# First stage: seven subtractions from VectorE to GpSimd, and transposes between the tiles on TensorE

## The chip, the cores and the metric

One NeuronCore of a Trainium2 chip runs the whole program. The metric is the device time in microseconds. The kernel before took 994.47 us (median of 3 runs, 994.19 to 994.80).

## The reference

The input is x, 2048 rows by 576 columns, f32. It is normalized over each row, goes through a 2-D real Fourier transform, is multiplied with complex weights, transformed back and added to x; then comes a second normalization, a wide layer of 4608 with ReLU, and a second addition.

```python
def _A_ref(x, w_r, w_i):
    X = jnp.fft.rfft2(x, axes=(-2, -1))
    X = X * (w_r + 1j * w_i)
    return jnp.fft.irfft2(X, s=(S, D), axes=(-2, -1))
def _B_ref(x, w1, w2):
    h = jnp.einsum("bsd,df->bsf", x, w1)
    return jnp.einsum("bsf,fd->bsd", jnp.maximum(h, 0), w2)
h = x + _A_ref(_layernorm(x), A_w_r, A_w_i)
h2 = h + _B_ref(_layernorm(h), B_w1, B_w2)
```

## The kernel before, in words

The rows are 16 tiles of 128 x 576. The program is written out in order, and each engine runs its instructions in the order in which they stand. There are four stages: the first (0 to 41 us of the span) normalizes, folds and makes the first step of the transform; the middle one (41 to 104 us) finishes the forward transform, multiplies and begins the inverse; then come the inverse with the second normalization, and the wide layer, nearly all of it matmuls.

The first stage is what the change touches. Its tiles go in 11 groups (`parts`, L237): tiles 0 to 3 alone, then the pairs 4-5, 6-7, 8-9, 10-11 and 12-13, then 14 and 15 alone. The steps of a group g are:

- `stat1` (L239, `ln_stats` L211): VectorE takes bn_stats (L215) and bn_aggr (L216) of x; GpSimd makes mean and scale out of them with three kinds of small instructions (L218 add, L219 power, L221 multiply, one for each tile). Below these are called the statistics block of a group.
- `norm1` (L243): ScalarE writes the normalized tile z (L229).
- `fold` (L251): VectorE adds z to its mirror image (L258, columns 1 to 288 of the buffer G), subtracts (L259, columns 289 to 576), and doubles column 0 by adding it to itself (L260).
- `fwd_a` (L264), for each tile: TensorE runs 12 matmuls (24 instructions in the trace, since each f32 matmul is done in two) into a PSUM buffer `d`, of which there are four. The first 4 matmuls (h = 0) read G's columns 0 to 255, all from the addition and the doubling; the next 4 (h = 1) read columns 320 to 575, from the subtraction; the last 4 (`rest`) read columns 256 to 319, from both. ScalarE copies the result to the buffer `A` (`act`, L158).

The loop at L301 sets the order: for g it writes stat1(g + 3), fold(g + 1), norm1(g + 2), then fwd_a of g's tiles. So on GpSimd the statistics block of g + 3 stands ahead of whatever fold(g + 1) puts there. Ahead of the loop stand 36 transposes of the identity (`warm_pe`, L289, L292), of which nothing is read; 8 and 12 more stand at the end of the middle stage. `mm` (L155) is the helper of all matmuls up to the inverse, so most of them have line L155. When the middle stage has read `A` for the last time, x is loaded again into the same memory (L449).

Of the kernel before, what the change touches and what calls it, by code (L numbers as in the profile page):

```python
# [13 lines left out]
ALU = mybir.AluOpType  # L14
# [14 lines left out]
GW = D + 2  # L29
# [93 lines left out]
def dims(ap, off, *pairs):  # L123

    return bass.AP(tensor=ap.tensor, offset=ap.offset + off, ap=[list(ap.ap[0]), *[list(p) for p in pairs]])
# [3 lines left out]
def kernel(ctx: ExitStack, tc: tile.TileContext, x, w_r, w_i, w1, w2, cc2, c1, fb, ib, c3, out):  # L129
    nc = tc.nc  # L130
# [5 lines left out]
    def sb(shape, tag, bufs=1, dt=F32):  # L136
        n[0] += 1
        return pool.tile(shape, dt, tag=tag, name=f"{tag}_{n[0]}", bufs=bufs)
# [3 lines left out]
    def ps():  # L142
        n[0] += 1
        if banks:
            return banks[0].tile([128, 1024], F32, tag="w", name=f"w_{n[0]}", bufs=2)
        return psum.tile([128, 1024], F32, tag="d", name=f"d_{n[0]}", bufs=4)
# [3 lines left out]
    def ebuf(shape, dt=F32):  # L150
        e = sb([128, EW], "e", EB, dt)[:, :int(np.prod(shape[1:]))]
        return e.rearrange("p (a b) -> p a b", a=shape[1]) if len(shape) == 3 else e

    def mm(o, l, r, start, stop):
        nc.tensor.matmul(o, l, r, start=start, stop=stop)  # L155

    def act(o, i, **kw):
        nc.scalar.activation(o, i, AF.Copy, **kw)  # L158
# [9 lines left out]
    ident = sb([128, 128], "ident")  # L168
# [82 lines left out]
    def fold(g):  # L251
        if g >= len(parts):
            return
        t0, k = parts[g]
        z = zin.pop(g)
        G = ebuf([128, 2, GW])
        a, b = dims(z, 1, [D, k], [287, 2], [1, 144]), dims(z, 575, [D, k], [-287, 2], [-1, 144])
        nc.vector.tensor_add(dims(G, 2, [GW, k], [-1, 2], [2, 144]), a, b)  # L258
        nc.vector.tensor_sub(dims(G, 575, [GW, k], [1, 2], [-2, 144]), a, b)  # L259
        nc.vector.tensor_add(G[:, :k, 0], z[:, :k, 0], z[:, :k, 0])  # L260
        for i in range(k):
            Fs[t0 + i] = G[:, i, :]

    def fwd_a(t):  # L264
        G = Fs.pop(t)
        p = ps()

        def rest(p):
            for e in range(2):
                for j in range(2):  # L270
                    q = slice(64 * j, 64 * j + 64)
                    mm(p[64 * e:64 * e + 64, 512 * j + 256:512 * j + 320], G[q, 256:320], caf[q, :64], True, True)

        end = t == NT - 1
        if end:
            p2 = ps()
            rest(p2)
            nc.vector.tensor_copy(dims(zx, 8192 + 2 * t, [32, 64], [1, 2]), dims(p2, 256, [1, 64], [512, 2]))
        for h in range(2):
            for k in range(2):  # L280
                for j in range(2):
                    q = slice(64 * j, 64 * j + 64)
                    mm(p[:, 512 * j + 128 * h:512 * j + 128 * h + 128], dims(G[q], (k, 321 - k)[h], [2, 128]),
                       caf[q, 64 * k:64 * k + 128], k == 0, k == 1)
        if not end:
            rest(p)
        act(dims(zx, 2 * t, [2048, 5 - end], [32, 64], [1, 2]), dims(p, 0, [64, 5 - end], [1, 64], [512, 2]))
# [9 lines left out]
    norm1(0)  # L297
    stat1(2)
    fold(0)
    norm1(1)  # L300
    for g in range(len(parts)):  # L301
        stat1(g + 3)
        fold(g + 1)
        norm1(g + 2)
        for t in range(parts[g][0], parts[g][0] + parts[g][1]):
            fwd_a(t)
# [844 lines left out]
```

## Time and profile before

| | us |
|---|---|
| median of 3 runs | 994.47 |
| the profiled execution's own time | 994.43 |
| its span, first to last instruction | 992.6 |
| TensorE busy, all stages | 972.9 |
| VectorE busy | 762.9 |
| ScalarE busy | 457.1 |
| GpSimd busy | 585.0 |
| first matmul of the middle stage starts at | 40.92 |
| in the first 41 us: TensorE, VectorE, ScalarE, GpSimd busy | 33.1, 28.1, 24.9, 19.5 |

PE is TensorE, DVE VectorE, ACT ScalarE, POOL GpSimd, SP the engine that issues most DMAs. In a row of the timeline stand the start, the duration, engine, line, operation, what is written and read, the count, and in brackets how long the engine was idle ahead of it and what ended that. PEclk is the granted clock of TensorE as a share of full speed.

### The profile page before, as it was taken

What the parts mean: (1) busy time and instruction counts of PE and PEld (TensorE: products, weight loads), DVE (VectorE), ACT (ScalarE), POOL (GpSimd) and SP (SyncE); (2) the same over time, 40 slices, a digit from 0 to 9 for tenths busy, and PEclk for the clock granted to TensorE, in tenths of its full rate; (3) what the DMA queues carried; (4) which work ended last, traced back from release to release, by engine and by line L of the source; (5) the groups of instructions that cost most, each with busy time, mean ns of one, the idle gap of its engine ahead of it and who ended that gap; (6) DMA issues with size and microseconds to landing.
All of it is one profiled execution on the core that took longest, in us unless ns stands there. A gap on an engine that the chain in (4) does not pass through costs nothing.

```text
span 992.6 us, 18029 instructions
## 1 busy us (share of the span) xinstructions
PE 972.9 (98%) x6708; PEld 863.1 (87%) x6708; DVE 762.9 (77%) x1185; ACT 457.1 (46%) x870; POOL 585.0 (59%) x730
## 2 busy tenths in 40 slices
PE   6999999999999999999999999999999999999997
PEld 6887668999998899999999999999999999999997
DVE  6688877437654878888888888878888888888886
ACT  5544364512323544544454554544454544544541
POOL 4300375602235867687767777687767777687741
PEclk8999999999999999999999999999999999999999
DMA  9952723466598472818264462819274563819365
GB/s 222 239 149 80 167 94 96 150 203 223 197 315 287 178 240 79 294 45 299 82 237 151 168 227 92 293 32 312 67 251 138 181 206 113 273 46 319 103 210 144
DMA packets 122727, 178.71 MB, mean 180 GB/s; under 512 B 7568, under 2 KB 102288, under 8 KB 122640
## 3 DMA queue, kind: packets, MB, share of 16 engines
q1 hardware_dynamic: 121904, 176.67, 55.4%
q8 instruction: 53, 0.87, 0.4%
q10 hardware_dynamic: 736, 0.89, 0.3%
q14 instruction: 34, 0.28, 0.1%
HBM read 153.15 MB, written 23.07 MB: 178 GB/s over the span
## 4 chain that ended last, share of the span: by engine, by line
PE 92%; DVE 4%; DMA 2%; ACT 1%; SPq 1%; issue 1%; DVEq 0%
PE h L784 33%; PE w L889 33%; PE d L155 24%; DMA A<-in_A_x_dram 2%; DVE st L215 1%; PE d L536 1%; PE w L155 1%; DMA X<-in_A_x_dram 1%; DVE A L899 0%; SPq L166 0%; DVE A L494 0%; PE h L889 0%; DVE D L600 0%; DVE mv L216 0%; ACT D L599 0%
## 5 line engine op out<-in xcount | busy, mean ns | idle before, releaser
L899 DVE TENSOR_TENSOR A<-A,w 128x576 f32<-128x576 f32 x415 | 307.3, 752 | 83.4 <-PE w L889 70.6
L889 PE MATMUL w<-X,D 128*128 128x288 f32 x1416 | 217.3, 295 | 0.5 <-ACT e L603 0.4
L889 PEld LDWEIGHTS w<-X,D 128*128 128x128 f32 x1416 | 204.4, 188 | 10.5 <-ACT e L603 0.6
L784 PE MATMUL h<-B,e 128*128 128x512 f32 x630 | 160.4, 393 | 0.9 <-DVE A L593 0.9
L158 ACT ACTIVATE e<-h 128x512 f32<-128x512 f32 x90 | 53.9, 599 | 184.4 <-PE h L784 184.4
L784 PEld LDWEIGHTS h<-B,e 128*128 128x128 f32 x630 | 113.3, 188 | 21.0 <-ACT e L158 1.1
L334 POOL TENSOR_TENSOR e<-e,e 128x512 fp32r<-128x512 f32 (+3 forms) x61 | 78.4, 1285 | 57.9 <-ACT e L158 52.7
L784 PE MATMUL h<-X,e 128*128 128x512 f32 x420 | 106.1, 392 | 0.0
L603 ACT ACTIVATE e<-e 128x512 f32<-128x512 f32 x90 | 57.0, 633 | 105.8 <-DVE e L842 46.6
L334 POOL TENSOR_TENSOR X<-e,X 128x576 fp32r<-128x576 f32 (+1 forms) x32 | 46.9, 1468 | 73.5 <-ACT X L158 73.5
L784 PEld LDWEIGHTS h<-X,e 128*128 128x128 f32 x420 | 75.7, 188 | 12.8
L158 ACT ACTIVATE e<-e 128x256 fp32r<-128x256 f32 (+5 forms) x162 | 74.5, 489 | 23.1 <-DMA t1T<-e 11.2
L808 POOL TENSOR_TENSOR A<-e 128x256 f32<-128x256 f32 x59 | 46.4, 787 | 27.4 <-DVE X L798 27.4
L798 DVE TENSOR_TENSOR D<-A,D 128x512 fp32r<-128x512 f32 x59 | 60.9, 1032 | 0.9 <-ACT D L158 0.9
L889 PEld LDWEIGHTS w<-X 128*128 128x128 f32 x360 | 53.8, 188 | 5.6 <-issue 0.7
L889 PE MATMUL w<-X 128*128 128x288 f32 x360 | 57.0, 294 | 0.5 <-DVE A L899 0.5
L889 PE MATMUL w<-X,e 128*128 128x288 f32 x348 | 55.5, 295 | 0.0
L155 PE MATMUL d<-e,D 128*128 128x288 f32 x384 | 53.4, 296 | 0.0
L155 PEld LDWEIGHTS d<-e,D 128*128 128x128 f32 x384 | 52.4, 188 | 1.1 <-issue 0.2
L784 PE MATMUL h<-C,e 128*128 128x512 f32 x210 | 53.3, 393 | 0.0
L784 PE MATMUL h<-F,e 128*128 128x512 f32 x210 | 53.2, 392 | 0.0
L810 POOL TENSOR_TENSOR A<-e,A 128x256 f32<-128x256 f32 x59 | 51.2, 868 | 0.8 <-DVE A L806 0.8
(164 smaller groups left out, 1863.3 us busy)
## 6 DMA issues: line engine op xcount, KB each, us to landing
X<-t0T SPq DMA_DIRECT2D x16, 768.0 KB, 8.0
X<-t1T SPq DMA_DIRECT2D x16, 768.0 KB, 7.8
e<-in_B_w_dram SPq DMA_DIRECT2D x18, 576.0 KB, 3.8
e<-in_B_w_dram SPq DMA_DIRECT2D x18, 512.0 KB, 3.9
X<-t0T SPq DMA_DIRECT2D x16, 512.0 KB, 8.6
X<-t1T SPq DMA_DIRECT2D x16, 512.0 KB
B<-t0T SPq DMA_DIRECT2D x8, 768.0 KB
F<-t0T SPq DMA_DIRECT2D x8, 768.0 KB
```

The costliest lines, as they stand in the source:

```text
L155: nc.tensor.matmul(o, l, r, start=start, stop=stop)
L158: nc.scalar.activation(o, i, AF.Copy, **kw)
L215: nc.vector.bn_stats(st[:, i, h, :], xs[:, t0 + i, 288 * h:288 * h + 288])
L334: eng.tensor_sub(l, v, h)
L536: nc.tensor.transpose(pz[:, 128 * ORDER[b]:128 * ORDER[b] + 128], y[:, 128 * b:128 * b + 128], ident)
L603: nc.scalar.activation(o, i, AF.Relu)
L784: nc.tensor.matmul(o, a, b, start=bool(first) and n_ == 0, stop=n_ == len(ops) - 1, skip_group_check=not first)
L798: (eng or nc.vector).tensor_sub(f[1], v, f[0])
L808: nc.gpsimd.tensor_sub(s3, p0[:, :256], p0[:, 256:])
L810: nc.gpsimd.tensor_sub(s4, p1_[:, :256], s2)
L889: nc.tensor.matmul(P[tt], l[:, q], r, start=first and n_ == 0, stop=end and n_ == 2, skip_group_check=whole and not first)
L899: nc.vector.tensor_add(xt, xt, P)
```

## The change

The subtraction of a fold goes to GpSimd in the first seven groups (tiles 0 to 9) and stays on VectorE in the other four. Column 0 is doubled by a multiplication with 2.0, which now stands ahead of the subtraction. And ahead of the matmuls of each of the tiles 1 to 11, TensorE gets four transposes of the identity into columns of the tile's PSUM buffer that nothing reads.

```diff
         nc.vector.tensor_add(dims(G, 2, [GW, k], [-1, 2], [2, 144]), a, b)
-        nc.vector.tensor_sub(dims(G, 575, [GW, k], [1, 2], [-2, 144]), a, b)
-        nc.vector.tensor_add(G[:, :k, 0], z[:, :k, 0], z[:, :k, 0])
+        nc.vector.tensor_scalar(G[:, :k, 0], z[:, :k, 0], 2.0, None, op0=ALU.mult)
+        (nc.gpsimd if g < 7 else nc.vector).tensor_sub(dims(G, 575, [GW, k], [1, 2], [-2, 144]), a, b)
         for i in range(k):
             Fs[t0 + i] = G[:, i, :]
...
+        if 1 <= t < 12:
+            for _ in range(4):
+                nc.tensor.transpose(p[:, 320:448], ident, ident)
         end = t == NT - 1
```

On GpSimd, before, the statistics blocks of the pairs 6-7 (r_284), 8-9 (r_318) and 10-11 (r_352) follow each other:

```order
L218 TENSOR_SCALAR r_284<-mv_283 128x2
L219 TENSOR_TENSOR r_284<-r_284,half_143 128x2
L221 TENSOR_SCALAR r_284<-mv_283,r_284 128x1 x2
L218 TENSOR_SCALAR r_318<-mv_317 128x2
L219 TENSOR_TENSOR r_318<-r_318,half_143 128x2
L221 TENSOR_SCALAR r_318<-mv_317,r_318 128x1 x2
L218 TENSOR_SCALAR r_352<-mv_351 128x2
```

After, at the same place (pair 6-7 is r_288, 8-9 r_326, 10-11 r_364; L260 is now the subtraction, e_299 the folded tile 3, e_337 the folded pair 4-5):

```order
L218 TENSOR_SCALAR r_288<-mv_287 128x2
L219 TENSOR_TENSOR r_288<-r_288,half_143 128x2
L221 TENSOR_SCALAR r_288<-mv_287,r_288 128x1 x2
L260 TENSOR_TENSOR e_299<-e_266 128x2x144
L218 TENSOR_SCALAR r_326<-mv_325 128x2
L219 TENSOR_TENSOR r_326<-r_326,half_143 128x2
L221 TENSOR_SCALAR r_326<-mv_325,r_326 128x1 x2
L260 TENSOR_TENSOR e_337<-e_303 128x2x2x144
L218 TENSOR_SCALAR r_364<-mv_363 128x2
```

Between every two statistics blocks there is now a subtraction, and the subtraction of tile 3 stands ahead of the block of 8-9, that of 4-5 behind it.

On TensorE, before, tiles 2 and 3 (d_302, d_336), with what each waits for:

```order
L155 MATMUL d_302<-cc_75,e_262 128x128 [waits DVE_49]
L155 MATMUL d_302<-cc_75,e_262 128x128 x7
L155 MATMUL d_302<-cc_75,e_262 64x64 x4
L155 MATMUL d_336<-cc_75,e_295 128x128 [waits DVE_49,PE_49]
L155 MATMUL d_336<-cc_75,e_295 128x128 x7
L155 MATMUL d_336<-cc_75,e_295 64x64 x4
```

After, the last of tile 3 (d_344) and tile 4 (d_382):

```order
L155 MATMUL d_344<-cc_75,e_299 128x128 [waits Pool_49]
L155 MATMUL d_344<-cc_75,e_299 128x128 x3
L155 MATMUL d_344<-cc_75,e_299 64x64 x4
L276 MATMUL d_382<-ident_64 128x128 [waits Activation_49]
L276 MATMUL d_382<-ident_64 128x128 x3
L155 MATMUL d_382<-cc_75,e_337 128x128 [waits DVE_49]
L155 MATMUL d_382<-cc_75,e_337 128x128 x3
L155 MATMUL d_382<-cc_75,e_337 128x128 [waits Pool_49]
L155 MATMUL d_382<-cc_75,e_337 128x128 x3
L155 MATMUL d_382<-cc_75,e_337 64x64 x4
```

A tile's matmuls now wait twice: the first four for VectorE, the other eight for GpSimd; the four transposes (L276) wait only for a free PSUM buffer. On VectorE the subtraction is gone from seven folds, so that the statistics of the next group follow the addition at once.

## The prediction

> **What bounds the kernel now.** I read the chain of waits in order of time first, then the windows of the first 95 us, then the timeline of the first stage engine by engine. The chain (start, duration, what) runs through the first stage and on:
>
> ```profile
> 21.66 73.62 PE d L155 x1093
> ...
> 95.30 0.66 SPq L449
> ...
> 97.71 5.80 DMA A<-in_A_x_dram
> ```
>
> From 21.66 us to 95 us it is TensorE without a break, and then the second load of x, which waits for TensorE. The middle stage alone (columns: window, length, then PE, PEld, DVE, ACT, POOL busy, clock, DMA):
>
> ```profile
> 41.00:95.00 54.00, 54.00 (x808) 42.64 (x810) 42.80 (x81) 22.75 (x68) 0.00 (x0) 1.00 0.50 136
> ```
>
> TensorE is busy 54.00 of 54.00 us there at full clock, so there is no slack: whatever the end of the first stage moves, the second load of x and the rest move too. The whole question is when the first stage's last matmuls end, 40.92 us before.
>
> TensorE alone in steps of 3.41 us (length, PE busy, clock, DMA):
>
> ```profile
> 6.80:10.21 3.41, 1.92 (x21) 1.00 1.05 240
> 10.21:13.63 3.42, 2.40 (x44) 1.00 1.02 232
> 13.63:17.04 3.41, 1.49 (x24) 1.00 1.05 238
> 17.04:20.45 3.41, 2.37 (x24) 0.50 1.03 230
> 20.45:23.87 3.42, 2.34 (x32) 0.50 1.03 241
> 23.87:27.28 3.41, 3.41 (x38) 0.50 1.02 305
> 27.28:40.92 13.64, 13.64 (x238) 1.00 0.89 212
> ```
>
> The clock is halved from 17.04 to 27.28 us. A window 44% busy (1.49) stands ahead of the fall, one 56% busy (1.92) did not bring it; 69% busy at half clock did not lift it, 100% did. What half clock costs is read from ScalarE's copies, one behind each tile (tiles 4, 5, then 12, 13), and from TensorE's own rows:
>
> ```profile
> 24.22 0.76 ACT L158 ACTIVATE A<-d 128x640 f32<-128x640 f32 x1 [0.31 <-PE d L155]
> 26.65 0.73 ACT L158 ACTIVATE A<-d 128x640 f32<-128x640 f32 x1 [1.67 <-PE d L155]
> ...
> 36.95 0.76 ACT L158 ACTIVATE A<-d 128x640 f32<-128x640 f32 x1
> 38.38 0.73 ACT L158 ACTIVATE A<-d 128x640 f32<-128x640 f32 x1 [0.68 <-PE d L155]
> ```
>
> ```profile
> 15.25 1.49 PE L155 MATMUL d<-cc,e 64*128 64x128 f32 x24 [2.33 <-DVE e L260]
> 18.08 2.50 PE L155 MATMUL d<-cc,e 64*128 64x128 f32 x24 [1.34 <-DVE e L260]
> 21.66 19.33 PE L155 MATMUL d<-cc,e 64*128 64x128 f32 x288 [1.08 <-DVE e L260]
> ```
>
> A tile takes 26.65 - 24.22 = 2.43 us at half clock and 38.38 - 36.95 = 1.43 us at full. Tiles 2, 3 and 4 begin when the fold is done (L260); from tile 4 on TensorE never waits. So two things could be won: an earlier start of tile 4, and about 2.3 tiles at 1.0 us less each.
>
> **The change, part by part.** *Transposes.* The 36 of the start, and the 8 and 12 of the middle stage's end:
>
> ```profile
> 3.40:6.80 3.40, 3.40 (x18) 3.40 (x17) 1.00 1.01 239
> 6.80:8.20 1.40, 1.34 (x12) 1.10 (x10) 1.00 1.10 262
> ```
>
> ```profile
> 100.11 1.09 PE L292 MATMUL d<-ident 128*128 128x128 f32 x8
> ...
> 102.92 1.53 PE L292 MATMUL d<-ident 128*128 128x128 f32 x12
> ```
>
> (1.53 - 1.09) / 4 = 0.11 us for one more at full clock, 3.40 / 18 = 0.19 us ahead of 6.8 us (the clock column shows 1.00 there, the spacing tells of a slower one). So four cost 0.45 us, or 0.76 when slow. Those of tiles 1 to 4 lie in waits for the folds and cost nothing as long as TensorE waits; those of tiles 5 to 11 stand between tiles that TensorE runs without a wait today: 7 x 0.45 = 3.1 us on the path. A tile with its four costs 1.43 + 0.45 = 1.88 us. This is more than the 2.3 us that a full clock gives back.
>
> *VectorE* loses the subtraction (L259, 0.45 us of a single tile, 0.76 us of a pair). The pair 4-5 before:
>
> ```profile
> 19.69 0.21 DVE L216 BATCH_NORM_AGGREGATE mv<-st 128x2 f32<-128x12 f32 x1
> 19.82 0.71 DVE L258 TENSOR_TENSOR e<-e 128x576 f32<-128x576 f32 x1
> 20.56 0.76 DVE L259 TENSOR_TENSOR e<-e 128x576 f32<-128x576 f32 x1
> 21.35 0.16 DVE L260 TENSOR_TENSOR e<-e 128x2 f32<-128x2 f32 x1
> ```
>
> The doubling as a multiplication I put at the same 0.16 us (between 0 and the 0.71 us of the addition; off the path, VectorE has slack afterwards).
>
> *GpSimd* gets seven subtractions. What else stands in its queue at this place, beside the rows above, and the same statistics block later, with no two-input VectorE instruction beside it:
>
> ```profile
> 15.80 0.50 POOL L221 TENSOR_SCALAR r<-mv,r 128x1 f32<-128x1 f32 x2
> ...
> 20.06 0.54 POOL L218 TENSOR_SCALAR r<-mv 128x2 f32<-128x2 f32 x1 [1.03 <-DVE mv L216]
> 20.68 1.20 POOL L219 TENSOR_TENSOR r<-r,half 128x2 f32<-128x2 f32 x1
> 21.98 0.50 POOL L221 TENSOR_SCALAR r<-mv,r 128x1 f32<-128x1 f32 x2
> ...
> 122.64 0.23 POOL L218 TENSOR_SCALAR r<-mv 128x2 f32<-128x2 f32 x1 [1.44 <-DVE mv L216]
> 122.96 0.73 POOL L219 TENSOR_TENSOR r<-r,half 128x2 f32<-128x2 f32 x1
> 123.79 0.50 POOL L221 TENSOR_SCALAR r<-mv,r 128x1 f32<-128x1 f32 x2
> ```
>
> A block takes 124.29 - 122.64 = 1.65 us alone and 22.48 - 20.06 = 2.42 us beside the fold: L218 ends only when L258 has, L219 is longer by the part of L259 that runs beside it. The reverse is also there, GpSimd first and VectorE waiting for its end (64 x 289, 0.46 us elsewhere):
>
> ```profile
> 100.75 0.46 DVE L402 TENSOR_TENSOR e<-e 64x289 f32<-64x289 f32 x1
> 100.89 0.86 POOL L402 TENSOR_TENSOR e<-e 64x289 f32<-64x289 f32 x1
> ...
> 101.23 0.83 DVE L401 TENSOR_TENSOR e<-e 64x289 f32<-64x289 f32 x1
> ```
>
> GpSimd ends at 101.75, and VectorE's second one 0.31 us later. So an addition and a subtraction of the fold exclude each other. The price of a subtraction, by the nearest groups (mean ns behind the busy us):
>
> ```profile
> L334 POOL TENSOR_TENSOR X<-e,X 128x576 fp32r<-128x576 f32 x31 | 44.5, 1438 | 73.5 <-ACT X L158 73.5
> ...
> L515 POOL TENSOR_TENSOR X<-e 128x287 f32<-128x287 f32 x16 | 14.2, 890 | 25.0 <-PE d L536 12.4 <-DMA A<-in_A_x_dram 6.8 <-DVE e L513 5.8
> ...
> L737 POOL TENSOR_TENSOR e<-e 128x288 f32<-128x288 f32 x15 | 12.1, 807 | 1.1
> ```
>
> I take 0.81 us for a tile and 1.44 us for a pair. The bounds are VectorE's 0.45 and 0.76 us from below, 0.89 and 2 x 0.89 = 1.78 us from above. [...]
>
> *The sum.* GpSimd, gaps of 0.1 us: the block of 4-5 ends at 15.80 + 0.50 = 16.3 as before; subtraction of tile 2 16.4 to 17.2; block of 6-7, 1.65 + 0.3 for tile 3's addition, 17.3 to 19.25; subtraction of tile 3 to 20.15; block of 8-9 from 20.25 (its statistics end by 19.90), 1.65 + 0.6, since L218 and the addition of 4-5 are both released by that subtraction's end: to 22.5; subtraction of 4-5 22.6 to **24.05** us. Before, this pair was ready at 21.5. From here a pair costs GpSimd 0.6 + 1.65 + 1.44 + 0.2 = 3.9 us: 6-7 at 27.95, 8-9 at 31.85.
> TensorE, at full clock: transposes and first third of tile 4 are done; its rest (two thirds, 0.95 us) ends at 25.0, tile 5 at 26.9, tile 6 waits and ends at 28.9, tile 7 at 30.8, tile 8 at 31.85 + 0.95 = 32.8, tiles 9 to 11 at 32.8 + 3 x 1.88 = 38.45, tiles 12 to 15 at 38.45 + 4 x 1.43 = 44.15. Against 40.92 this is 3.2 us later, so 994.43 + 3.2 = **997.6 us** (the profiled execution lies 0.04 under the median of the runs).
>
> **The rivals.** *The exclusion costs little.* If blocks and subtractions run at 1.65 and 1.44 whatever VectorE does, 4-5 is ready at 23.15, TensorE is the bound, and the end is 23.15 + 0.95 + 7 x 1.88 + 4 x 1.43 = 43.0: 996.5 us. Against it are the rows of 2.42 and 0.83.
> *The clock falls once more.* From 20.45 to 23.87 TensorE would have the end of tile 3, four transposes and a third of tile 4, 1.65 us or 48%, between the 44% and the 56% above. At half clock to 27.28 it loses 3.41 x (1 - 1.43/2.43) = 1.4 us, of which GpSimd's lateness hides some 0.4: 998.6 us.
> *The transposes do not hold the clock*, so the change doesn't do what it is built for. Then each tile from 4 to 11 costs 2.43 + 0.76 = 3.2 us, with matmuls 76% of it, and only tiles 12 and 13 at 2.43 lift the clock: 24.05 + 1.6 + 7 x 3.2 + 2 x 2.43 + 2 x 1.43 = 55.8, 1009 us. Against it: behind the 36 transposes of the start, where the spacing went from 0.19 to 1.40 / 12 = 0.12 us, the first tiles ran at full clock. [...]
> *Faster: GpSimd keeps up and the transposes lie in TensorE's waits.* At VectorE's prices and without exclusion 4-5 is ready at 19.5 + 0.1 + 1.65 + 0.76 = 22.0 (19.5: the statistics of 8-9 end at 19.90 less half of the 0.8 us of two subtractions that went from in front of them), and with transposes free the end is 22.0 + 0.95 + 11 x 1.43 = 38.7: 992.2 us. It decides at 21.1 us for the pair 4-5 with the transposes paid, at 24.2 with all of them hidden and 2.86 us for a pair on GpSimd. For it speak only TensorE's waits for L260; a block and a subtraction need 3.1 us by the rows.
>
> **How the numbers follow.** Forecast 0.45, little exclusion 0.21, clock falls 0.25, transposes don't hold the clock 0.04, faster 0.05. The range: down to 995.8 (little exclusion, and the three subtractions ahead of tile 4's end half way to VectorE's price, 0.18 + 0.18 + 0.34 = 0.7 less), up to 999.0 (clock falls, and 0.13 us for a transpose, 0.4 more). A difference of 0.2%, 2.0 us, is about what a measurement of this kernel can tell from none. Faster by more: 0.05. Within: half of the second case and a little of the first, 0.13. Slower: 0.82.
>
> **What would show it.** In the profile after: subtractions of 1.4 us or more on GpSimd; the last two thirds of tile 4 released by GpSimd near 24 us; VectorE's additions of pairs idle or stretched to over 1 us; clock 1.00 from 24 us on; tiles 9 to 11 spaced 1.88 us; the middle stage beginning near 44 us and its length unchanged. It is wrong if 4-5 is ready before 22 us, if copies of tiles 5 to 11 stand 1.5 us apart (transposes free), or if the stages behind 44 us change their length.

## The result, and the profile after

The changed kernel takes 996.09 us (median of 12 runs, 995.78 to 996.92), the kernel before 994.25 us on the same chip (12 runs, 993.08 to 995.61): a ratio of 1.0021, 95% interval 1.0013 to 1.0029. The forecast was 3.2 us more; it is 1.8 by the medians. The direction and the range held, the size did not.

The profiled execution's span is 994.0 us, and its middle stage begins at 42.35 us. Behind that point nothing moved: 994.0 - 42.35 = 951.65 us, against 992.6 - 40.92 = 951.68 before. In all profiles of this study this rest is 951.4 to 951.9 us, so the start of the middle stage measures each of them.

TensorE in the same windows as before the change (length, PE busy, clock, DMA):

```profile
13.63:17.04 3.41, 2.79 (x39) 1.00 1.01 238
17.04:20.45 3.41, 3.12 (x40) 1.00 1.04 245
20.45:23.87 3.42, 2.24 (x32) 1.00 1.00 268
23.87:27.28 3.41, 3.41 (x52) 1.00 1.06 275
```

The clock is full where it was halved. TensorE's timeline, from the first third of tile 4 on:

```profile
19.87 0.74 PE L155 MATMUL d<-cc,e 64*128 64x128 f32 x8
21.80 1.02 PE L155 MATMUL d<-cc,e 64*128 64x128 f32 x16 [1.18 <-POOL e L260]
22.74 0.66 PE L276 MATMUL d<-ident 128*128 128x128 f32 x4
23.33 1.50 PE L155 MATMUL d<-cc,e 64*128 64x128 f32 x24
24.76 0.66 PE L276 MATMUL d<-ident 128*128 128x128 f32 x4
25.34 1.49 PE L155 MATMUL d<-cc,e 64*128 64x128 f32 x24
...
35.39 7.03 PE L155 MATMUL d<-cc,e 64*128 64x128 f32 x120
42.35 3.34 PE L155 MATMUL d<-e,A 64*64 64x290 f32 x48
```

The rest of tile 4 is released by GpSimd (L260) at 21.80 us; from there TensorE never waits. Four transposes (L276) and the 24 matmul instructions alternate, each tile 25.34 - 23.33 = 2.01 us behind the last one, of which 23.33 - 22.74 = 0.59 us goes to the transposes. GpSimd's queue in the same stretch:

```profile
14.46 0.51 POOL L221 TENSOR_SCALAR r<-mv,r 128x1 f32<-128x1 f32 x2
14.92 0.80 POOL L260 TENSOR_TENSOR e<-e 128x288 f32<-128x288 f32 x1
...
17.48 0.80 POOL L260 TENSOR_TENSOR e<-e 128x288 f32<-128x288 f32 x1
18.38 0.60 POOL L218 TENSOR_SCALAR r<-mv 128x2 f32<-128x2 f32 x1
19.06 0.71 POOL L219 TENSOR_TENSOR r<-r,half 128x2 f32<-128x2 f32 x1
19.87 0.51 POOL L221 TENSOR_SCALAR r<-mv,r 128x1 f32<-128x1 f32 x2
20.33 1.41 POOL L260 TENSOR_TENSOR e<-e 128x576 f32<-128x576 f32 x1
21.83 0.60 POOL L218 TENSOR_SCALAR r<-mv 128x2 f32<-128x2 f32 x1
...
23.79 1.41 POOL L260 TENSOR_TENSOR e<-e 128x576 f32<-128x576 f32 x1
```

L260 is the subtraction, L218 to L221 a statistics block. A subtraction takes 0.80 us for a tile and 1.41 us for a pair. The block of 8-9, 18.38 to 20.38, takes 2.0 us, since L218 lasts 0.60 us instead of 0.23. A pair costs 23.79 - 20.33 = 3.46 us, less than TensorE's 2 x 2.01. VectorE's side of it:

```profile
11.08 0.82 DVE L215 BATCH_NORM_STATS2 st<-X 128x6 f32<-128x288 f32 x2 [0.95 <-DMA X<-in_A_x_dram]
...
20.99 1.36 DVE L258 TENSOR_TENSOR e<-e 128x576 f32<-128x576 f32 x1
22.39 0.17 DVE L259 TENSOR_SCALAR e<-e 128x2 f32<-128x2 f32 x1
```

An addition of 0.71 us lasts 1.36 us beside the subtraction of 20.33 to 21.74. And the first of these rows shows a thing that the kernel before's profile hid: the statistics of tiles 4 and 5, the last that wait for x, begin at 11.08 us here and began at 12.38 us there, though no part of the change touches the loading of x.

### The profile page after: what moved, and what is told of

It reads as the page before. It is cut to its first block, busy times and chain, and to the rows that moved or that the text cites. A ratio compares the mean times of both kernels' runs of the same rounds, so it can differ in the third digit from the quotient of the medians.

```text
span 994.0 us, 18102 instructions
## 1 busy us (share of the span) xinstructions
PE 977.1 (98%) x6752; PEld 865.4 (87%) x6752; DVE 763.4 (77%) x1178; ACT 456.6 (46%) x870; POOL 591.4 (59%) x737
## 4 chain that ended last, share of the span: by engine, by line
PE 92%; DVE 3%; DMA 2%; ACT 1%; SPq 1%; POOL 1%; issue 1%; DVEq 0%
PE h L787 33%; PE w L892 33%; PE d L155 24%; DMA A<-in_A_x_dram 2%; PE d L539 1%; PE w L155 1%; DVE st L215 1%; DMA X<-in_A_x_dram 1%; DVE A L902 0%; PE d L276 0%; SPq L166 0%; DVE A L497 0%; PE h L892 0%; DVE D L603 0%; POOL e L260 0%
```

## The experiments

Two theories stood against each other. **A**: the loss is the transposes of tiles 5 to 11 on TensorE's path, at 0.59 us for four, and the subtraction on GpSimd is nearly free. **B**: the loss is the late subtraction, and the transposes lie in waits. Ratios are to the kernel before, with their 95% intervals. x is the start of the statistics of tiles 4 and 5 (in the rows with 11.32 and 11.28 x had landed before VectorE came to it), all in us.

| kernel | x | tile 4, or its rest, starts | middle stage starts | ratio |
|---|---|---|---|---|
| before | 12.38 | 21.66 | 40.92 | |
| changed | 11.08 | 21.80 | 42.35 | 1.0021 (1.0013 to 1.0029) |
| transposes only | 11.32 | 20.50 | 41.53 | 1.0025 (1.0016 to 1.0034) |
| GpSimd only | 11.16 | 21.84 | 40.55 | 1.0006 (0.9997 to 1.0015) |
| transposes ahead of 1 to 4, GpSimd | 11.21 | 21.90 | 40.13 | 1.0008 (0.9999 to 1.0017) |
| transposes ahead of 1 to 4, VectorE | 11.28 | 20.46 | 39.39 | 0.9997 (0.9988 to 1.0006) |
| eight transposes | 11.44 | 22.14 | 45.75 | one run |
| doubling alone | 11.05 | 19.52 | 40.02 | one run |
| fold first, 1 to 4, GpSimd | | 19.64 | 38.65 | 0.9992 (0.9983 to 1.0000) |
| fold first, 1 to 4, VectorE | | 19.41 | 40.57 | 1.0006 (0.9997 to 1.0015) |
| fold first, GpSimd, none | | 20.17 | 39.23 | 0.9990 (0.9981 to 0.9999) |

**Transposes only.** The kernel before with these lines:

```diff
+        if 1 <= t < 12:
+            for _ in range(4):
+                nc.tensor.transpose(p[:, 320:448], ident, ident)
```

> The kernel before with the four transposes ahead of tiles 1 to 11; all subtractions stay on VectorE. Theory A (four transposes cost 0.59 us on TensorE's path for each of the tiles 5 to 11, the subtraction on GpSimd is nearly free): tile 4 starts at 20.3 to 21.6 us, as x lands, tile and transposes take 2.01 us, the middle stage begins at 41.5 to 42.8 us, total 1 to 2 us over the kernel before. Rival B (the loss is GpSimd's, the transposes lie in waits): the middle stage begins at 40 us, total 1 us under the kernel before.

Measured: 995.80 us against 993.48, 2.3 us over and so a little more than A's 1 to 2, and the middle stage at 41.53 us. TensorE:

```profile
20.50 1.49 PE L155 MATMUL d<-cc,e 64*128 64x128 f32 x24 [1.51 <-DVE e L260]
21.92 0.65 PE L276 MATMUL d<-ident 128*128 128x128 f32 x4
22.51 1.50 PE L155 MATMUL d<-cc,e 64*128 64x128 f32 x24
...
41.53 3.34 PE L155 MATMUL d<-e,A 64*64 64x290 f32 x48
```

Tile 4 is done at 21.92 us, 0.8 us sooner than in the changed kernel (22.74), since its subtraction stayed on VectorE; by the same 0.8 us the middle stage begins sooner (41.53 against 42.35). The step to tile 5 is 22.51 - 20.50 = 2.01 us again. By the ratios (1.0025 and 1.0021) the transposes alone give the whole loss; by these two profiles the subtraction's move adds 0.8 us to it. B falls as the whole of it.

**GpSimd only.** The changed kernel without those lines.

> The changed kernel without the transposes: seven subtractions on GpSimd, doubling by a multiplication. Theory A: tile 4 can go on at 21.7 us; if the clock falls in the waits as in the kernel before, the middle stage begins at 41 us and the total is within 0.5 us of the kernel before; if it stays full, at 40.3 us with GpSimd the bound, 0.7 us under. Rival B: 1 to 2 us over the kernel before, as the whole change.

Measured: 994.14 against 993.48 us, not told apart from the kernel before, and the middle stage at 40.55 us. The clock fell again:

```profile
13.63:17.04 3.41, 2.03 (x36) 0.99 1.02 238
17.04:20.45 3.41, 2.88 (x28) 0.50 1.04 243
...
23.87:27.28 3.41, 3.41 (x38) 0.51 1.07 282
```

**Transposes only ahead of tiles 1 to 4**, with GpSimd, and then with all subtractions on VectorE:

```diff
-        if 1 <= t < 12:
+        if 1 <= t < 5:
```

> The changed kernel with the transposes only ahead of tiles 1 to 4, where TensorE waits anyway. Theory A: the clock stays full, tiles 5 to 15 go at 1.43 us or at GpSimd's pace of 3.5 us a pair up to tile 8, the middle stage begins at 40.3 us, total 2 us under the changed kernel and 0.5 us under the kernel before. Rival B: as the changed kernel.

> The kernel before with the transposes only ahead of tiles 1 to 4; all subtractions stay on VectorE. Theory A: the clock stays full, VectorE's folds are the bound up to tile 13 (ready at 34.5 us, then 4 tiles of 1.43), the middle stage begins at 39.3 to 40.2 us, total 0.7 to 1.5 us under the kernel before. Rival B: 0 to 1 us under it as well; it differs from A only together with the run of the transposes alone.

Measured: 994.06 and 993.16 us. In both profiles the clock is full (1.00 in every window) from tile 0 to the end of the stage, so four transposes in each of the first waits were enough for that. With GpSimd:

```profile
21.90 3.12 PE L155 MATMUL d<-cc,e 64*128 64x128 f32 x48 [1.18 <-POOL e L260]
25.35 3.12 PE L155 MATMUL d<-cc,e 64*128 64x128 f32 x48 [0.33 <-POOL e L260]
29.36 10.83 PE L155 MATMUL d<-cc,e 64*128 64x128 f32 x184 [0.89 <-POOL e L260]
40.13 3.34 PE L155 MATMUL d<-e,A 64*64 64x290 f32 x48
```

With VectorE:

```profile
20.46 2.92 PE L155 MATMUL d<-cc,e 64*128 64x128 f32 x48 [1.51 <-DVE e L260]
24.56 2.92 PE L155 MATMUL d<-cc,e 64*128 64x128 f32 x48 [1.18 <-DVE e L260]
28.16 11.30 PE L155 MATMUL d<-cc,e 64*128 64x128 f32 x192 [0.67 <-DVE e L260]
39.39 3.34 PE L155 MATMUL d<-e,A 64*64 64x290 f32 x48
```

The brackets are the point: at full clock TensorE waits for the folds, 0.33 and 0.89 us in front of the rests of tiles 6 and 8 for GpSimd, 1.51, 1.18 and 0.67 us in front of 4, 6 and 8 for VectorE. A's 2 us between this and the changed kernel are there (42.35 - 40.13 = 2.2), but the gain over the kernel before that I expected (0.5, and 0.7 to 1.5 us) is not: a full clock buys little when the folds come at this pace. The two runs also price the move of the subtraction to GpSimd (and of the doubling, which goes with it): 994.06 against 993.16 us, and 40.13 against 39.39 for the middle stage, so 0.7 to 0.9 us. In this order of the loop A's "nearly free" does not hold.

**Eight transposes** in place of four, otherwise the changed kernel.

> The changed kernel with eight transposes instead of four ahead of tiles 1 to 11. Theory A (all of a transpose's time is on TensorE's path from tile 5 on): four more cost 4 x 0.11 = 0.45 us a tile if the 0.59 us of the first four hold 0.14 us of change between the two forms of matmul, 0.59 us if each takes 0.147; a tile then stands 2.46 or 2.60 us behind the last one, and the middle stage begins 3.1 to 4.1 us later than in the changed kernel, near 45.5 to 46.5 us. Rival B (transposes lie in waits): under 1 us later.

Measured: 999.29 us in the one run, and the middle stage 3.4 us later than in the changed kernel.

```profile
23.09 1.09 PE L276 MATMUL d<-ident 128*128 128x128 f32 x8
24.11 1.50 PE L155 MATMUL d<-cc,e 64*128 64x128 f32 x24
25.54 1.09 PE L276 MATMUL d<-ident 128*128 128x128 f32 x8
...
45.75 2.47 PE L155 MATMUL d<-e,A 64*64 64x290 f32 x34
```

A tile takes 25.54 - 23.09 = 2.45 us, 0.44 more: 0.11 us for a transpose. The remaining 0.59 - 0.44 = 0.15 us is paid once for a group of transposes; that the change between the two forms of matmul is its cause was not tried apart. Seven groups make 7 x 0.44 = 3.1 of the 3.4 us, and 0.3 is the later start of tile 4's rest (22.14 against 21.80).

**The doubling alone**, the kernel before with

```diff
+        nc.vector.tensor_scalar(G[:, :k, 0], z[:, :k, 0], 2.0, None, op0=ALU.mult)
         nc.vector.tensor_sub(dims(G, 575, [GW, k], [1, 2], [-2, 144]), a, b)
-        nc.vector.tensor_add(G[:, :k, 0], z[:, :k, 0], z[:, :k, 0])
```

> The kernel before with column 0 doubled by a multiplication ahead of the subtraction, nothing else; at the same time a second look at the first stage as it was. All theories: no difference from the doubling (0.15 us either way). If the late x of the kernel before's one profile (statistics of tiles 4 and 5 from 12.38 us) was that execution's alone, they begin at 11.0 to 11.4 us here, the clock is halved for 10 us all the same, and the middle stage begins at 39.2 to 40.0 us instead of 40.92; if it was the kernel's, at 12.4 and 40.9.

Measured: 993.53 us in the one run, beside 993.43 for the kernel before. VectorE, then the windows of TensorE:

```profile
11.05 0.82 DVE L215 BATCH_NORM_STATS2 st<-X 128x6 f32<-128x288 f32 x2 [0.15 <-DMA X<-in_A_x_dram]
```

```profile
10.21:13.63 3.42, 2.33 (x32) 0.62 1.05 251
...
23.87:27.28 3.41, 3.41 (x38) 0.50 1.06 275
27.28:40.92 13.64, 13.64 (x232) 0.97 0.93 222
```

and TensorE from tile 4 on beside VectorE's subtraction of that pair:

```profile
19.52 20.57 PE L155 MATMUL d<-cc,e 64*128 64x128 f32 x288 [0.66 <-DVE e L259]
```

```profile
19.41 0.76 DVE L260 TENSOR_TENSOR e<-e 128x576 f32<-128x576 f32 x1
```

x is there at 11.05 us. By the shares of 0.62 and 0.97 in the outer windows the clock is at half from 11.02 to 28.09 us, 17 us in place of the 10 in the kernel before's profile, and yet the middle stage begins at 40.02 us, 0.9 us sooner than in that profile. Not all of that is x. L259 is here the doubling, and with it ahead of the subtraction the first third of tile 4 starts at 19.52 us without waiting for the subtraction, which ends at 20.17; in the runs with the old order tile 4 starts behind the whole fold (20.46 and 20.50). So the doubling's place, for which I had expected no difference, starts this tile some 0.65 us sooner (20.17 - 19.52), and this is not quite a second profile of the kernel before; in the time of the one run no gain shows.

That 40.92 is late is shown rather by the times of the kernel before: less the same rest (994.43 - 40.92 = 953.51 us), the medians of the later comparisons, 993.19 to 993.48, put its middle stage at 39.7 to 40.0 us, and the 994.25 of the comparison with the changed kernel at 40.7. The step of the changed kernel from this profile is 2.3 us.

**The fold ahead of the statistics.** In the loop, with transposes ahead of tiles 1 to 4, on GpSimd and on VectorE; the third kernel has no transposes between tiles and GpSimd's subtractions:

```diff
-        stat1(g + 3)
         fold(g + 1)
+        stat1(g + 3)
         norm1(g + 2)
```

> Transposes ahead of tiles 1 to 4, seven subtractions on GpSimd, and in the loop fold(g + 1) ahead of stat1(g + 3), so that a subtraction stands ahead of the statistics block on GpSimd. If tile 4's end was late because its subtraction stood behind the block of tiles 8 and 9, it comes 1.5 to 2 us sooner than 21.7, the pace of 3.5 us a pair stays, and the middle stage begins at 38.5 us, 1 to 1.5 us under the kernel before in total. If what binds is VectorE's and ScalarE's chain, it begins at 40 us as with the old order.

> Transposes ahead of tiles 1 to 4, all subtractions on VectorE, and fold(g + 1) ahead of stat1(g + 3). Control for the other run with this order: if the gain there is the order's alone, the middle stage begins 0.5 to 1.5 us sooner here than with the old order (39.4 us); if it needs GpSimd, it is the same or later, since VectorE waits for the normalized tile.

> Seven subtractions on GpSimd, fold(g + 1) ahead of stat1(g + 3), no transposes between the tiles. If the gain of that order needs the clock that the transposes ahead of tiles 1 to 4 hold, the clock falls in the waits here (half for 10 to 17 us), the middle stage begins 1 to 2 us later than the 38.65 us with them, and the total is that of the kernel before or more. If the supply of folds alone sets the end, it begins at 38.6 to 39.2 us whatever the clock does, and the total stays about 1 us under the kernel before.

Measured: 992.43, 993.96 and 992.50 us, against 993.43, 993.43 and 993.19. The first one's TensorE:

```profile
19.64 3.12 PE L155 MATMUL d<-cc,e 64*128 64x128 f32 x48 [0.75 <-POOL e L260]
23.51 3.12 PE L155 MATMUL d<-cc,e 64*128 64x128 f32 x48 [0.74 <-POOL e L260]
27.19 9.57 PE L155 MATMUL d<-cc,e 64*128 64x128 f32 x160 [0.55 <-POOL e L260]
37.23 1.49 PE L155 MATMUL d<-cc,e 64*64 64x64 f32 x24 [0.47 <-DVE e L260]
38.65 3.34 PE L155 MATMUL d<-e,A 64*64 64x290 f32 x48
```

The rest of tile 4 is released 2.3 us sooner than with the old order (19.64 against 21.90). GpSimd's subtraction of that pair, which had stood behind the statistics block of 8-9 and begun at 20.43 us, is now ahead of it:

```profile
18.18 1.41 POOL L260 TENSOR_TENSOR e<-e 128x576 f32<-128x576 f32 x1
```

The pairs then follow 3.9 and 3.7 us apart (23.51 - 19.64, 27.19 - 23.51), not the 3.5 that I expected to stay. On VectorE the same order starts tile 4 1.05 us sooner too (19.41 against 20.46), but the stage ends 1.2 us later (40.57 against 39.39), so the gain at the end needs the subtraction on GpSimd. The third one, TensorE's windows:

```profile
10.21:13.63 3.42, 2.52 (x26) 0.66 1.05 248
13.63:17.04 3.41, 3.41 (x52) 0.84 1.01 241
...
20.45:23.87 3.42, 3.42 (x46) 0.66 1.01 241
23.87:27.28 3.41, 3.41 (x52) 0.84 1.04 296
```

Here the clock falls twice for 3.4 us each, every time across two of these windows (0.66 and 0.84), not for the 10 to 17 us that I had named; the middle stage begins 0.6 us later, and the total, 0.7 us under the kernel before, cannot be told from the first one's. Of my two cases the one by the supply of folds is the nearer. These two kernels are the best of the study, by 0.1% or a little less, at the edge of what the measurement can tell.

## Why the prediction was right in its direction and too large

- *Only the start of the middle stage counts.* Right: 951.65 against 951.68 us.
- *Seven groups of transposes at 0.45 us.* Mis-sized: 0.59 us, 7 x 0.59 = 4.1 instead of 3.1. The rows that I used were runs of 8 and 12 transposes, in whose difference the 0.15 us that come once with a group cannot appear.
- *The price of a subtraction, 0.81 and 1.44 us.* Right: 0.80 and 1.41.
- *Addition and subtraction exclude each other.* Right in kind, seen on both engines (0.60 in place of 0.23, 1.36 in place of 0.71 us); a block beside a pair's addition takes 2.0 us, 0.35 more than the 1.65 of the block at 122.64 us, not 0.6. That block was not alone, as I had put it: L494, with the two inputs `A` and `d`, ran beside it on VectorE from 122.47 to 123.87 us.
- *Tile 4's pair ready at 24.05 us, then 3.9 us a pair, and GpSimd the bound to tile 8.* This is the step that failed, and by the prediction's own sign: it was to be wrong if this pair was ready before 22 us. It was ready at 21.74, 2.3 us sooner. Of these, 1.3 is the start: the block of 4-5 ended at 14.97 instead of 16.3, because x came sooner than in the one profile that I worked from; 1.0 is the chain from there, 6.77 us instead of 7.75, spread over all of its steps (0.15 to 0.25 us less for each subtraction with its gap and each block). At 3.46 us a pair GpSimd keeps ahead, and TensorE, with 2.01 us a tile, is the bound from tile 5 on. From 21.80, 0.95 + 7 x 2.01 + 4 x 1.42 = 20.7 us give 42.5; 42.35 was measured.
- *The clock.* It stayed full, as in the forecast. The window of 20.45 to 23.87 was 2.24 of 3.42 us busy, not 48%, as tile 4's rest came sooner. Halving was no small risk: a window 60% busy (2.03 of 3.41 us) stands ahead of the fall in the GpSimd-only run.
- *The comparison.* I set 44.1 against 40.92. By the medians of its times the kernel before's stage ends near 40.7 in this comparison and near 40.0 in the later ones. So the same late execution put both sides of the difference too late, and the transposes, too cheap by 1.0 us, stand against a chain too long by 1.0 us: that the range held is in part luck.

The rival in which the exclusion costs little (996.5 us) came nearest to 996.09, with TensorE as the bound, which is what happened. Its reason, no exclusion, is not what the rows show, and its 43.0 us for the stage is close to 42.35 also because its cheap transposes make up in part for its late start. The rival in which the transposes don't hold the clock is refuted: in all seven profiles with transposes ahead of tiles 1 to 4 the clock stays full through the stage (1.00 in every window of 3.41 us), in all four without it fell to 0.50. (A profile is one execution. The mean granted clock of the changed kernel's 12 runs is 0.996 to 1.000 over the whole program, beside 0.992 to 0.996 in the kernel before's later ones; 0.996 is some 8 us at half clock by my estimate, 2 x 0.004 x 994 us, and where they lie in the runs without a profile is not known.)

Where did the expected gain go? A full clock is worth 1.0 us on each of two to four tiles (1.43 in place of 2.43 us) only if TensorE is the bound. At full clock a pair takes it 2 x 1.43 = 2.86 us, while folds come every 3.4 to 4.0 us (GpSimd: 25.35 - 21.90, 29.36 - 25.35) or 3.6 to 4.1 us (VectorE: 28.16 - 24.56, 24.56 - 20.46), so the gain turned into waits, and the transposes of tiles 5 to 11 filled these and 2.2 us more.

VectorE's 3.6 us for a pair is its own work without a gap: in the run with transposes ahead of 1 to 4 and all subtractions on VectorE, 24.33 to 26.30 us are the statistics of two tiles and 26.30 to 28.01 a fold. In the pair with 4.1 us bn_aggr (L216) waits 0.51 us more, which the profile puts down to GpSimd's L221.

Open: the kernel before was profiled once, with late x, and what makes x late there was not tried, nor why its median is 994.25 us beside the changed kernel and 993.19 to 993.48 later. How much of the changed kernel's own loss is the subtraction's move is not settled either: 0.8 us by two profiles, none by the ratios.

## What to carry to other kernels

Work that keeps the clock up, here four transposes ahead of each of tiles 1 to 4, belongs only into waits that are there at full clock; between tiles without a wait the same instructions were paid in full, 0.11 us for each and 0.15 us more for a group. Before a slower engine takes over a step (GpSimd took 1.41 us for a pair's subtraction, VectorE 0.76), look at what stands ahead of it in that engine's queue: here the order in one loop was worth more than the move (40.13 - 38.65 = 1.5 us at the start of the middle stage, against 40.13 - 39.39 = 0.7). And a sum made against one execution inherits its accidents; see which waits for DMA are in it.

## What the runs showed of the hardware

In the four profiles in which the clock fell, it was at half for 10.24 us in the kernel before (17.04 to 27.28 us) and in GpSimd only (17.00 to 27.24), 17.07 in doubling alone (11.02 to 28.09) and twice 3.42 in fold first without transposes (11.32 to 14.74, 21.56 to 24.98), that is 3, 3, 5, 1 and 1 times 3.41; the two falls of the last stand 10.24 us apart, again 3 times 3.41. Counted from the start of the span, the falls of different profiles are no whole number of such steps apart: from 11.02 (doubling alone) to 17.04 us (kernel before) it is 1.8.

In steps of 3.41 us counted from the profile's own fall, the step ahead of a fall is busy for 28% and 62% (fold first, none, 0.95 and 2.13 us), 44% (kernel before, 1.49 us), 56% (doubling alone, 1.92 us) and 60% (GpSimd only, 2.03 us). But 56% in the kernel before (6.80 to 10.21 us, also 1.92 us) and 62% in GpSimd only (6.76 to 10.17 us, 2.11 us) brought no fall, so in these profiles a busy share between 56% and 62% decides nothing by itself. Nor did one full step at half clock always lift it: in doubling alone two follow each other (21.26 to 24.68 and 24.68 to 28.09 us), and only behind the second did the clock rise.
